# Scores of batches 2 and 3 as float32 products in row tiles, in a fused attention and feed-forward kernel

## The chip, the cores and the metric

The kernel runs on one core of one Trainium2 chip. The metric is the device time of one execution in microseconds (us). Before the change it is 682.39 us, the median of 3 runs (682.06, 682.39, 684.04). One further execution was profiled; all rows below are from it.

## The reference

Attention with 4 batches, 8 heads, 576 positions and 64 dimensions a head, and then a feed-forward layer over all 2304 tokens (512 wide, 2048 hidden):

```python
scores = np.matmul(q, k.transpose(0, 1, 3, 2)) / np.sqrt(D)
x = log1p(abs(i - j)) / log1p(max(i, 1))               # per pair of positions
scores += (np.maximum(x * w1 + b1, 0) @ w2)             # a bias per head, the same for all batches
attn = softmax(scores)                                  # over keys
x = concat_heads(attn @ v)                              # 2304 x 512
h = x @ w_in
out = (h * sigmoid(h)) @ w_out
```

All inputs but the two feed-forward weights are float32; those are float64 and are narrowed to float32 on the chip.

## The kernel before, in words

**Stages.** Work is handed out by a planner (class `Plan`, from line 202 on): every operation has a kind, an assumed duration on each engine that can do it, a due time, and the buffers it reads and writes. The due time is a time worked out from the stage's constants plus an offset from the table `SHIFT` (line 40), one for each group's loads, matmuls and other operations. The planner runs a list schedule once, in Python, and so fixes the order of the instructions on each engine. On TensorE it adds `KEEP` (1.5 us, line 214) to the due time of an operation whose kind needs the array in another mode than the last one (`MODES`, same line: the value product, the bias product, `s_row` and `s_quad` each have a mode of their own; all others share one).

Stage 1 (to about 167 us of the profiled span) builds the position bias and does attention of batches 0 and 1. Stage 2 (about 167 to 372 us) does attention of batches 2 and 3, mixed with the feed-forward steps of the first 384 tokens (`ff_block`) and the narrowing and splitting of their weights. After it come the rest of `ff_block` and three blocks of 512 tokens with a Strassen-like scheme (`ff_super`).

**Attention of one chunk** (`chunk`, line 746). For a batch, a pair of heads and 128 query positions there are two score tiles of 128 x 576, one for each head (a fifth chunk of 64 positions is done by `s_quad`, line 756, in all batches). A score tile takes two of the eight PSUM banks, and the pool for them has two slots. VectorE then adds the bias and takes the maximum (L795), ScalarE the exponential (L802), TensorE transposes (L811, 9 in a chunk, in a run of 4 and one of 5), ScalarE or VectorE copies the result out, and once in a visit of some chunks TensorE multiplies with the values (L683).

**The two ways to a score tile.** For batches in `RAW` (line 25: 0 and 1) keys are loaded once (352 KB for a pair of heads, `keys`, line 587), so that the lower 64 partitions hold the first half of the keys and the upper 64 the second half; queries stand twice. `s_row` (line 775, L779) multiplies float32 data as loaded, each half of the partitions by itself:

```python
for hf, y in enumerate(HALF):                 # partitions 0-63, 64-127
    T.matmul(out=s[:, hf, 0:288], lhsT=tl(qst)[y, ...128 columns], rhs=tl(kst)[y, ...288], ...)
```

The trace shows 4 matmul records of 64 rows for such a tile (each product is two records, and the records of the two halves start together).

For batches 2 and 3 keys are loaded as 576 KB, twice over the partitions. They are rounded to a shorter format (`k_hi`, line 599, ScalarE or VectorE, L446 or L448), and the rest is taken by a subtraction (`k_lo`, line 604, two for a pair of heads, GpSimd or VectorE, L451). Queries likewise: `q_hi` on all partitions (line 629), `q_lo` on the upper half (line 633). `s_mm` (line 783, L788) then does four products over all 128 rows:

```python
for hf in range(2):
    for j, part in enumerate((khi, klo)):
        T.matmul(out=s[:, hf, 0:288], lhsT=tl(qs)[:, ...128], rhs=tl(part)[:, ...288], start=(j == 0), stop=(j == 1))
```

Batches 2 and 3 have 64 such tiles (2 batches, 4 pairs of heads, 4 chunks, 2 heads), and so have batches 0 and 1.

**Feed-forward steps beside them.** L867 multiplies by `w_in` (128 x 384), L890 by `w_out` (128 x 512), both in the same mode as `s_mm` and the transposes. L974 and L1058 are those of `ff_super`.

Of the kernel before, what the change touches and what calls it, by code (L numbers as in the profile page):

```python
# [24 lines left out]
RAW, QUAD, WL = (0, 1), (0, 1, 2, 3), 36.0  # L25
# [10 lines left out]
def f(ap):  # L36
# [4 lines left out]
    0: -7.0, 1: 7.2, 2: -8.7, 4: -10.5, 5: -14.0, 6: -14.7, 8: -19.2, 9: -21.0, 10: -18.6, 12: -17.2,  # L41
    13: -18.5, 14: -9.8, 16: -16.4, 17: -6.4, 18: 4.7, 20: -8.1, 21: -11.7, 22: 12.8, 24: -5.2, 25: -7.1,
    26: 1.7, 28: -3.1, 29: -26.7, 30: 5.4, 32: -4.9, 33: -23.7, 34: -10.8, 36: -9.6, 37: -16.1, 38: -12.7,
    40: -6.4, 41: -8.3, 42: -11.4, 44: -24.3, 45: -29.4, 46: -28.2, 48: -5.1, 49: -9.3, 50: -0.5, 52: -23.9,
    53: -23.5, 54: -16.7, 56: -27.5, 57: -25.7, 58: -20.1, 60: 4.1, 61: -0.1, 62: 3.8, 64: 8.7, 65: 8.1,
    66: -1.9, 68: 7.8, 69: 14.7, 70: 8.1, 72: 12.6, 73: 16.4, 76: 14.4, 77: 10.2, 78: 11.6, 80: 4.6, 81: -24.7,
    82: 3.1, 84: -3.2, 85: 0.7, 86: -3.2, 88: 4.3, 89: -24.8, 90: 7.1, 92: -9.1, 93: -34.8, 94: -8.7, 96: -7.4,
    97: -22.8, 98: -22.1, 100: -13.1, 101: -10.2, 102: -9.7, 104: -0.8, 105: -0.4, 106: 2.5, 108: 1.7,
    109: 2.6, 110: 6.6, 112: 18.1, 113: 3.1, 114: 9.0, 116: 1.1, 117: -8.2, 118: -0.3, 120: -0.2, 121: -12.5,
    122: -0.4, 124: -7.9, 125: -12.6, 126: -17.3, 128: -4.0, 129: -5.3, 130: -3.7, 132: 2.8, 133: -15.5,  # L50
    134: 5.0, 136: 9.3, 137: -19.5, 138: 0.8, 140: -2.8, 141: -29.5, 142: -8.8, 144: 2.8, 145: -20.9,
    146: -22.4, 148: 8.1, 149: -12.1, 150: 14.7, 152: -14.5, 153: -7.5, 154: -4.7, 156: -0.6, 157: -2.7,
    158: 17.0, 160: -0.2, 161: -16.4, 162: 1.7, 164: -9.4, 165: -33.7, 166: 1.4, 168: -4.2, 169: -5.6,
    170: -0.1, 172: -3.4, 173: -15.3, 174: 1.8, 176: 6.5, 177: -24.9, 178: 0.9, 180: 9.8, 181: -2.1, 182: -0.4,
    184: -12.2, 185: -3.7, 186: -1.6, 188: 6.7, 189: -13.5, 190: -2.5, 192: 16.8, 193: -0.9, 194: 3.1,
    196: -0.1, 197: -9.5, 198: 5.1, 200: -5.4, 201: 0.7, 202: -0.1, 204: 4.2, 205: 5.5, 206: 12.7, 208: 8.0,
    209: 7.5, 210: 7.6, 212: 15.4, 213: 4.0, 214: 13.2, 216: 7.3, 217: 1.0, 218: 4.4, 220: -0.3, 221: -2.4,
    222: -0.8, 224: 5.9, 225: -0.1, 226: -11.2, 228: 5.7, 229: -5.8, 230: -4.1, 232: 2.7, 233: -1.6, 234: 3.1,
    236: 9.4, 237: -7.4, 238: -0.8, 240: 5.1, 241: 0.3, 242: 3.7, 244: 1.2, 245: -0.9, 246: 6.3, 248: -8.9,
    249: -8.9, 250: 7.7, 252: 3.9, 253: -8.6, 254: 5.4, 256: 7.0, 257: 0.4, 258: 12.5, 260: 2.3, 261: -1.5,  # L60
    262: -0.8, 264: 9.9, 265: -5.1, 266: 6.9, 268: 0.4, 269: -10.9, 270: -8.1, 272: 13.8, 273: -9.7, 274: 12.1,
    276: -19.9, 277: -14.6, 278: -14.1, 280: -9.1, 281: -5.9, 282: -6.8, 284: 9.7, 285: -3.1, 286: -3.8,
    288: 22.2, 289: 1.6, 290: -0.2, 292: 37.9, 293: -6.4, 294: -4.8, 296: 17.7, 297: -0.1, 298: -3.5, 300: 0.5,
    301: -11.1, 302: -6.6, 304: 13.0, 305: -18.6, 306: -2.9, 308: 9.4, 309: -2.2, 310: -3.1, 312: 13.1,
    313: -10.3, 314: -10.4, 316: 21.4, 317: 5.4, 318: -7.1, 320: -2.1, 321: -1.5, 322: -11.3, 324: 10.8,
    325: -1.6, 326: -3.4, 328: 12.6, 329: 7.1, 330: -4.9, 332: 3.7, 333: 10.8, 334: 13.6, 336: -3.8, 337: -2.4,
    338: -4.1, 340: -2.8, 341: -15.1, 342: -14.3, 344: -8.7, 345: -7.9, 346: 3.5, 348: -4.7, 349: -5.6,
    350: -0.2, 352: 8.1, 353: -3.2, 354: 10.4, 356: -3.5, 357: -5.5, 358: 1.3, 360: 4.2, 361: -2.3, 362: 4.3,
    364: -7.4, 365: -12.4, 366: -16.2, 368: -7.2, 369: -7.2, 370: -3.2, 372: 6.7, 373: 6.6, 374: 7.2,
    376: -28.6, 377: -8.5, 378: -3.2, 380: -21.8, 381: -29.9, 382: -25.2, 384: 5.4, 385: -3.5, 386: 2.6,  # L70
    388: -6.5, 389: 6.7, 390: -8.6, 392: 5.7, 393: -3.5, 394: -1.1, 396: -2.4, 397: -2.0, 398: -1.8, 400: 8.0,
    401: 13.3, 402: 8.4, 404: 16.0, 405: 1.9, 406: 5.4, 408: -11.5, 409: -5.9, 410: -11.7, 412: -7.6,
    413: -4.7, 414: -7.6, 416: -11.0, 417: -27.1, 418: -8.5, 420: -19.9, 421: -39.2, 422: -24.3, 424: 11.0,
    425: 9.8, 426: 10.4, 428: 5.5, 429: -4.9, 430: -0.8, 432: 0.4, 433: -23.5, 434: -2.0, 436: -5.2, 437: -5.4,
    438: -4.3, 440: 3.4, 441: 4.3, 442: -6.2, 444: 5.7, 445: 4.9, 446: -3.4, 448: 10.8, 449: 2.8, 450: -4.7,
    452: -10.7, 453: -13.0, 454: 8.2, 456: 16.5, 457: 2.6, 458: 10.4, 460: 1.9, 461: 3.0, 462: 1.6, 464: 13.9,
    465: 8.4, 466: 11.0, 468: 10.2, 469: 10.3, 470: 11.8, 472: 10.5, 473: 1.0, 474: 1.0, 476: 12.5, 477: 8.7,
    478: 2.3, 480: -2.4, 481: -12.5, 482: -2.7, 484: 2.0, 485: -4.3, 486: 0.2, 488: -4.9, 489: 1.5, 490: 9.4,
    492: -6.3, 493: -5.6, 494: -7.4, 496: -2.5, 497: -0.3, 498: 1.8, 500: -12.0, 501: 1.0, 502: 1.2, 505: -0.6,
    506: 1.1, 508: 7.2, 509: -4.1, 510: 0.2, 512: 1.9, 513: 1.5, 514: 6.1, 516: -15.9, 517: -15.0, 518: 4.6,  # L80
    520: -15.3, 521: -1.1, 522: 17.7, 524: -3.6, 525: -6.2, 526: 2.9, 528: 6.9, 529: -5.3, 530: 4.2,
    532: -18.5, 533: 14.7, 534: 19.5, 536: -4.2, 537: 2.7, 538: -6.9, 540: -5.7, 541: 2.2, 542: 5.2, 544: 9.5,
    545: -15.8, 546: -10.5, 548: 7.8, 549: 0.5, 550: 2.7, 552: -18.8, 553: -0.7, 554: 5.7, 556: 7.1, 557: 3.6,
    558: 7.0, 560: 23.0, 561: -1.7, 562: 1.1, 564: -6.5, 565: 3.8, 566: -6.5, 568: 1.6, 569: 0.5, 570: 20.2,
    573: -1.7, 574: -4.9, 576: 2.7, 577: -4.8, 578: -9.9, 580: 8.2, 581: 5.1, 582: -4.4, 584: 2.1, 585: -1.8,
    586: -5.8, 588: -5.7, 589: 4.1, 590: -4.6, 592: -13.8, 593: -3.1, 594: -1.9, 596: 7.8, 597: 9.7, 598: 9.0,
    600: -4.2, 601: -0.8, 602: -2.9, 604: 6.2, 605: 0.7, 606: 0.7, 608: 6.9, 609: 4.0, 610: 7.5, 612: 2.4,
    613: -0.9, 614: 6.6, 616: 11.8, 617: 3.8, 618: 0.1, 620: 15.7, 621: -5.2, 622: 16.3, 624: -2.4, 625: -3.2,
    626: 1.4, 628: 21.2, 629: 8.1, 630: 13.9, 632: 10.8, 633: 6.0, 634: 10.8, 636: 4.1, 637: 4.0, 638: -0.5,
    640: 1.9, 644: 3.4, 645: -4.7, 646: -4.0, 648: 8.4, 649: 6.6, 650: 1.6, 652: -6.4, 653: 2.1, 654: -4.1,  # L90
    656: -2.7, 657: 8.5, 658: -1.2, 660: 4.6, 661: 4.7, 662: 3.6, 664: 9.2, 665: 8.7, 666: 15.6, 668: 1.3,
    669: 3.3, 670: 4.6, 672: -1.5, 673: 2.4, 674: 9.3, 676: 4.4, 677: -2.5, 678: -0.7, 680: 0.7, 681: -1.0,
    682: -1.4, 684: 3.2, 685: -1.5, 686: -1.0, 688: -7.6, 689: 1.7, 690: -5.8, 692: 8.5, 693: 12.6, 694: 6.4,
    696: 3.9, 697: 1.3, 698: 1.6, 700: 21.6, 701: 0.7, 702: 11.1, 704: 9.4, 705: -0.6, 706: 3.6, 708: 5.9,
    709: 5.3, 710: 6.8, 712: 3.5, 713: 5.9, 714: 6.9, 716: -2.1, 717: -2.3, 718: -0.5, 720: -1.6, 721: -5.3,
    722: 0.8, 724: 0.4, 725: 0.4, 726: 4.4, 728: -4.5, 729: 6.0, 730: 6.2, 732: 14.3, 733: 18.6, 734: 20.5,
    736: 5.7, 737: 1.2, 738: -2.5, 740: 2.9, 741: 5.1, 742: 2.2, 744: -0.8, 745: 10.7, 746: 4.6, 748: -0.3,
    749: -2.7, 750: 4.0, 752: -2.8, 753: 2.1, 754: 26.5, 756: 7.7, 757: 7.6, 758: 5.6, 760: 3.6, 761: 6.3,
    762: 3.5, 764: 2.8, 765: 7.4, 766: 7.2, 768: 6.9, 769: 4.6, 770: -3.6, 772: 12.4, 773: -0.7, 774: 6.0,
    776: -12.5, 777: 0.1, 778: -3.7, 780: 9.9, 781: 6.1, 782: -2.0, 784: 15.1, 785: -1.0, 786: 7.2, 788: -0.8,  # L100
    789: -0.7, 790: -0.4, 792: 13.9, 793: 12.9, 794: 14.7, 796: 8.7, 797: 10.3, 798: -13.5, 800: -2.5,
    801: 5.6, 802: -1.3, 804: 7.8, 805: 16.3, 806: 17.2, 808: -10.1, 809: -10.5, 810: -6.5, 812: -8.0,
# [1183 lines left out]
```

## Time and profile before

| | |
|---|---|
| median of 3 runs | 682.39 us |
| the profiled execution | 683.77 us, of which the span of instructions 681.8 us |
| granted TensorE clock | 1.00 in every slice |
| busy share of the span | TensorE 98%, its weight loads 83%, VectorE 83%, ScalarE 62%, GpSimd 18% |
| moved by DMA | 186 MB, 274 GB/s |

A busy TensorE says little here: matmul records overlap, and a record lasts longer than the next one waits. What a matmul costs is read from start to start. In the rows, "L788" is line 788 of the kernel, "PEld" a weight load, and "a<-b" the tile written and those read.

### The profile page before, as it was taken

The numbers are of one execution on the slowest core, as the hardware profiler recorded it, in microseconds if no ns is written. First come the engines' busy times: TensorE is split into PE (matmuls) and PEld (weight loads), VectorE is DVE, ScalarE is ACT, GpSimd is POOL, SyncE is SP. The second block draws the span as 40 slices with busy tenths as digits, with TensorE's granted clock in tenths as the row PEclk, the third lists the DMA queues.
The fourth block names the chain that finished last, engine by engine and source line by source line (L and its number), as shares of the span: only waits on it lengthen the run. The fifth ranks groups of instructions, "written<-read, shape, count | busy, mean of one in ns | idle before, by whom it ended". The sixth has DMA issues, their size and how long they took to land.

```text
span 681.8 us, 15118 instructions
## 1 busy us (share of the span) xinstructions
PE 669.7 (98%) x5500; PEld 568.5 (83%) x5500; DVE 567.8 (83%) x1240; ACT 423.6 (62%) x901; POOL 120.6 (18%) x119
## 2 busy tenths in 40 slices
PE   9899999999999999999999999999999999999997
PEld 5356767777878788787877899999999999999997
DVE  7899696788999998898977788988899566995775
ACT  8899685678898787697755346565574423632331
POOL 1000000204241222114303223230131000300120
PEclk9999999999999999999999999999999999999999
DMA  8989846788699874889547969899899888799921
GB/s 289 313 281 317 273 136 203 242 257 259 224 332 299 314 240 161 289 257 323 158 135 258 357 253 324 303 307 309 295 361 395 289 342 283 281 372 351 402 91 62
DMA packets 84073, 186.49 MB, mean 274 GB/s; under 512 B 11552, under 2 KB 34464, under 8 KB 84000
## 3 DMA queue, kind: packets, MB, share of 16 engines
q1 hardware_dynamic: 84000, 185.54, 79.3%
q8 instruction: 43, 0.70, 0.4%
q14 instruction: 30, 0.25, 0.1%
HBM read 139.93 MB, written 45.57 MB: 272 GB/s over the span
## 4 chain that ended last, share of the span: by engine, by line
PE 56%; DVE 2%; DMA 1%; ACT 1%; issue 0%; ACTq 0%; DVEq 0%
PE psum L1058 18%; PE psum L974 17%; PE psum L867 7%; PE psum L890 6%; PE psum L683 3%; PE psum L811 2%; PE psum L788 2%; DMA G<-win_d 1%; ACT G L802 0%; PE psum L762 0%; DVE G L451 0%; ACT G L446 0%; DVE G L1037 0%; ACT w L533 0%; DVE w L546 0%
## 5 line engine op out<-in xcount | busy, mean ns | idle before, releaser
L802 ACT ACTIVATE G<-G,sm 128x576 f32<-128x576 f32 (+1 forms) x144 | 111.5, 777 | 29.5 <-DVE sm L795 28.7
L1058 PE MATMUL psum<-G 128*128 128x256 f32 x864 | 119.2, 283 | 0.3 <-DVE G L451 0.3
L795 DVE CUSTOM_DVE_ANT_0 G<-psum,G 128x576 f32<-128x576 f32 (+1 forms) x144 | 105.4, 759 | 9.5 <-PE psum L788 4.0
L1058 PEld LDWEIGHTS psum<-G 128*128 128x128 f32 x864 | 110.5, 192 | 0.7 <-DVE G L451 0.5
L811 PEld LDWEIGHTS psum<-ident,G 128*128 128x128 f32 x656 | 73.0, 141 | 25.9 <-ACT G L802 8.6
L811 PE MATMUL psum<-ident,G 128*128 128x128 f32 x656 | 91.9, 277 | 1.6 <-ACT G L802 0.8
L683 PE MATMUL psum<-pt,M 128*64 128x128 f32 (+3 forms) x1120 | 85.8, 306 | 0.2 <-ACT pt L446 0.2
L974 PE MATMUL psum<-pt,G 128*128 128x256 f32 x576 | 81.1, 284 | 0.0
L683 PEld LDWEIGHTS psum<-pt,M 128*64 128x64 f32 x1120 | 62.0, 137 | 21.9 <-issue 3.9
L867 PE MATMUL psum<-M,G 128*128 128x384 f32 x384 | 76.4, 341 | 0.0
L890 PE MATMUL psum<-G,M 128*128 128x512 f32 x288 | 75.2, 398 | 0.0
L974 PEld LDWEIGHTS psum<-pt,G 128*128 128x128 f32 x576 | 74.3, 192 | 0.6 <-ACT M L446 0.2
L451 POOL TENSOR_TENSOR G<-w,G 128x512 fp32r<-128x512 f32 x27 | 36.1, 1345 | 184.7 <-ACT G L446 158.2
L446 ACT ACTIVATE pt<-psum 128x512 f32<-128x512 f32 (+3 forms) x100 | 51.7, 535 | 26.4 <-PE psum L811 20.1
L867 PEld LDWEIGHTS psum<-M,G 128*128 128x128 f32 x384 | 65.9, 188 | 2.3 <-issue 1.0
L448 DVE COPY pt<-psum 128x640 f32<-128x640 f32 (+3 forms) x92 | 53.9, 602 | 14.2 <-PE psum L811 8.5
L890 PEld LDWEIGHTS psum<-G,M 128*128 128x128 f32 x288 | 51.6, 188 | 9.9 <-issue 1.3
L446 ACT ACTIVATE G<-G 128x512 fp32r<-128x512 f32 (+1 forms) x56 | 38.0, 694 | 23.0 <-DVE G L1037 19.5
L1010 ACT ACTIVATE M<-M 128x512 f32<-128x512 f32 x24 | 15.2, 631 | 54.4 <-DVE M L1001 54.4
L446 ACT ACTIVATE G<-w 128x512 fp32r<-128x512 f32 x64 | 39.4, 625 | 11.3 <-DVE w L551 5.4
L788 PE MATMUL psum<-G,M 128*128 128x288 f32 x256 | 45.8, 309 | 0.4 <-DVE pt L448 0.2
L788 PEld LDWEIGHTS psum<-G,M 128*128 128x128 f32 x256 | 36.6, 188 | 7.4 <-DVE sm L795 2.2
(100 smaller groups left out, 1056.7 us busy)
## 6 DMA issues: line engine op xcount, KB each, us to landing
G<-ts_d SPq DMA_DIRECT2D x48, 512.0 KB, 5.6
G<-win_d SPq DMA_DIRECT2D x40, 512.0 KB, 6.7
G<-bias_d SPq DMA_DIRECT2D x32, 576.0 KB, 5.8
G<-us_d SPq DMA_DIRECT2D x32, 512.0 KB, 6.4
bias_d<-G SPq DMA_DIRECT2D x36, 295.5 KB, 5.2
G<-in_w_out_dram SPq DMA_DIRECT2D x16, 512.0 KB, 6.0
G<-in_w_in_dram SPq DMA_DIRECT2D x16, 512.0 KB, 5.1
win_d<-G SPq DMA_DIRECT2D x16, 512.0 KB, 5.5
```

The lines of the kernel that those rows point to most:

```text
L446: A.activation(out=out, in_=in_, func=AF.Copy)
L448: ENG[e].tensor_copy(out=out, in_=in_)
L451: ENG[e].tensor_tensor(out=out, in0=in0, in1=f(in1), op=ALU.subtract)
L683: T.matmul(out=tl(o)[x, d:d + n], lhsT=tl(vs)[:, (s + 1) % 5 * 128 + 64 * a:(s + 1) % 5 * 128 + 64 * a + 64], rhs=tl(pt)[:, s + 5 * a if s ...
L788: T.matmul(out=s[:, hf, 0:288], lhsT=tl(qs)[:, x0 + 128 * a:x0 + 128 * a + 128], rhs=tl(part)[:, S * a + 288 * hf:S * a + 288 * hf + 288], ...
L795: V.tensor_tensor_reduce(out=mine(p, a).rearrange("p (a n) -> p a n", a=2), in0=tl(sps[a]).rearrange("p (a n) -> p a n", a=2)[:, :, 0:widt ...
L802: A.activation(out=mine(p, a), in_=mine(p, a), func=AF.Exp, scale=-1.0, bias=tl(sm)[:, i + a:i + a + 1], accum_out=tl(sq)[:, col + 4 * a:c ...
L811: T.transpose(out=tl(tp)[:, 128 * s:128 * s + 128], in_=tl(p)[:, 128 * (s0 + s):128 * (s0 + s) + 128], identity=ident)
L867: T.matmul(out=tl(hp)[:, 0:TB], lhsT=tl(wr)[:, x, 128 * cc:128 * cc + 128], rhs=tl(xs[cc])[:, y, :], start=(cc + m == 0), stop=(cc == NC - ...
L890: T.matmul(out=tl(acc[i]), lhsT=tl(gg)[:, x, 128 * i:128 * i + 128], rhs=tl(wo[fi])[:, y, :], start=(fi == 0 and m == 0), stop=(fi == NF - ...
L974: T.matmul(out=half(i), lhsT=tl(w)[:, x, off + 128 * cc:off + 128 * cc + 128], rhs=tl(b)[:, at, y, :], start=(fresh and cc + n == 0), stop ...
L1058: T.matmul(out=tl(c)[:, 256 * i:256 * i + 256], lhsT=tl(g)[:, a, x + 128 * i:x + 128 * i + 128], rhs=tl(w)[:, b, y:y + 256], start=(fresh ...
```

## The change

Two things are edited. `RAW` now names all four batches, so that every branch on it goes the other way for batches 2 and 3: their keys are loaded in the 352 KB layout (also at the host, which lays out `k0` for `len(RAW)` batches), `k_hi`, `k_lo`, `q_hi` and `q_lo` aren't issued, `s_row` takes the place of `s_mm`, and `s_quad` reads the keys at the offsets of the other layout. And all offsets in `SHIFT` are new; the groups keep their numbers.

```diff
-RAW, QUAD, WL = (0, 1), (0, 1, 2, 3), 36.0
+RAW, QUAD, WL = (0, 1, 2, 3), (0, 1, 2, 3), 36.0
...
 SHIFT = {
-    0: -7.0, 1: 7.2, 2: -8.7, 4: -10.5, 5: -14.0, 6: -14.7, 8: -19.2, 9: -21.0, 10: -18.6, 12: -17.2,
...
+    0: -12.3, 1: 0.7, 2: -18.9, 4: -12.3, 5: -10.8, 6: -9.9, 8: -17.3, 9: -13.7, 10: -21.1, 12: -19.4,
...
 }
```

The branches that it turns, in `keys`, `queries` and `chunk`:

```python
if b in RAW:                                   # keys: one buffer, no split
    kst = buf("G", [128, 704]); load("ld_k", ..., in_=k0[b, hp]); return kst, kst, kst
if b in RAW or not n:                          # queries: as loaded
    return qst, qst
for a in range(2) if b in RAW else (): ...     # chunk: s_row
for a in range(2) if b not in RAW else (): ... # chunk: s_mm
```

## Rows read from the trace of the kernel before

**Rows 1.** The page: engines' busy time over the span, and TensorE's granted clock in 40 slices.
```profile
PE 669.7 (98%) x5500; PEld 568.5 (83%) x5500; DVE 567.8 (83%) x1240; ACT 423.6 (62%) x901; POOL 120.6 (18%) x119
...
PEclk9999999999999999999999999999999999999999
```

**Rows 2.** Busy time by stretch, stage 2: stretch, length, then engines, clock, DMA.
```profile
167.00:207.00 40.00, 39.77 (x350) 33.32 (x351) 38.94 (x89) 35.87 (x81) 15.46 (x15) 1.00 0.82 284
...
sum 205.00, PE 204.33 PEld 166.41 DVE 184.58 ACT 157.08 POOL 52.48; mean PE 40.87 PEld 33.28 DVE 36.92 ACT 31.42 POOL 10.49
```

**Rows 3.** Timeline of TensorE, stage 1: start, length, engine, line, operands, records.
```profile
90.19 1.20 PE L811 MATMUL psum<-ident,G 128*128 128x128 f32 x9
91.33 1.24 PE L779 MATMUL psum<-G,M 64*128 64x288 f32 x8
92.50 1.20 PE L811 MATMUL psum<-ident,G 128*128 128x128 f32 x9
```

**Rows 4.** Timeline of TensorE where stage 1 passes into stage 2.
```profile
166.85 0.76 PE L779 MATMUL psum<-G,M 64*128 64x288 f32 x4
167.53 0.80 PE L788 MATMUL psum<-G,M 128*128 128x288 f32 x4
168.17 1.15 PE L811 MATMUL psum<-ident,G 128*128 128x128 f32 x9
169.07 1.31 PE L788 MATMUL psum<-G,M 128*128 128x288 f32 x8
170.24 0.77 PE L811 MATMUL psum<-ident,G 128*128 128x128 f32 x5
```

**Rows 5.** Timeline of TensorE in stage 2, score tiles between feed-forward steps.
```profile
238.11 0.69 PE L788 MATMUL psum<-G,M 128*128 128x288 f32 x4
238.64 0.70 PE L867 MATMUL psum<-M,G 128*128 128x384 f32 x3
...
240.15 1.21 PE L788 MATMUL psum<-G,M 128*128 128x288 f32 x8
241.20 0.85 PE L890 MATMUL psum<-G,M 128*128 128x512 f32 x3
```

**Rows 6.** Timeline of TensorE in stage 2, score tiles behind a value product.
```profile
257.60 1.34 PE L788 MATMUL psum<-G,M 128*128 128x288 f32 x8
258.78 0.86 PE L890 MATMUL psum<-G,M 128*128 128x512 f32 x3
```

**Rows 7.** Timeline of TensorE, the first run of row-tiled score tiles.
```profile
44.69 1.62 PE L779 MATMUL psum<-G,M 64*128 64x288 f32 x8
```

**Rows 8.** Timeline of TensorE, the last run of split score tiles.
```profile
361.67 1.22 PE L788 MATMUL psum<-G,M 128*128 128x288 f32 x8
```

**Rows 9.** Groups by line and shape, whole span: count, busy, mean ns, idle before.
```profile
L446 ACT ACTIVATE G<-G 128x1152 fp32r<-128x1152 f32 x7 | 8.1, 1153 | 0.0
L451 DVE TENSOR_TENSOR G<-G 128x576 fp32r<-128x576 f32 x11 | 8.0, 750 | 0.0
L451 POOL TENSOR_TENSOR G<-G 128x576 fp32r<-128x576 f32 x5 | 7.0, 1424 | 4.8 <-PE psum L683 3.5 <-ACT G L446 1.2
L446 ACT ACTIVATE M<-M 128x512 fp32r<-128x512 f32 x11 | 6.9, 626 | 0.4 <-DMA M<-in_q_dram 0.4
L451 DVE TENSOR_TENSOR M<-M 64x512 fp32r<-64x512 f32 x9 | 6.3, 700 | 0.5 <-ACT M L446 0.3
L451 POOL TENSOR_TENSOR M<-M 64x512 fp32r<-64x512 f32 x7 | 10.1, 1447 | 27.6 <-ACT M L446 18.5 <-DMA M<-in_q_dram 5.0 <-PE psum L762 3.7
```

**Rows 10.** Timeline of TensorE in stage 2, its largest late start inside one mode.
```profile
348.88 1.51 PE L788 MATMUL psum<-G,M 128*128 128x288 f32 x8 [0.21 <-DVE pt L448]
350.22 0.69 PE L867 MATMUL psum<-M,G 128*128 128x384 f32 x3
```

**Rows 11.** DMA issues: count, KB each, median us to landing.
```profile
G<-in_k_dram SPq DMA_DIRECT2D x8, 576.0 KB, 5.6
```

**Rows 12.** The page: the chain that ended last, share of the span by engine.
```profile
PE 56%; DVE 2%; DMA 1%; ACT 1%; issue 0%; ACTq 0%; DVEq 0%
```

298 rows, old and new, of the table SHIFT are left out of this document.

## The prediction

> **What bounds the kernel now.** I read the page first: TensorE is busy 98% of the span at the full granted clock, 2.4 GHz, the next engine (VectorE) 83% [rows 1]. Then the stretches of stage 2, where the change lies: TensorE is without a record for 0.67 of 205 us; VectorE has 184.58 us there and is nearly full only at the start, 38.94 of 40 [rows 2]. Busy records overlap, though, so third I read TensorE's timeline from start to start, to see what one tile costs and what it costs to get into and out of it. In it nearly every record of stage 2 follows the one before at the usual step of its line. I counted the starts that come over 50 ns later than that line or that pair of lines usually has: 20 in stage 2; all lateness there, the small ones too, sums to 5.0 us. One is the pair of tiles at 348.88, which takes 1.34 us to the next start [rows 10] where 1.05 is usual [rows 5]. So stage 2 is bound by the sum of TensorE's steps, and its feed-forward work fills what attention leaves: a step more on TensorE is a later end, a step less on another engine is worth only the lateness that it caused.
>
> **The change part by part.**
>
> *The products.* 64 tiles of `s_mm` go, 64 of `s_row` come. `s_mm` between feed-forward steps takes 0.53 us for one tile (238.11 to 238.64) and 1.05 for two (240.15 to 241.20) [rows 5]. `s_row` takes 0.68 us alone (166.85 to 167.53) [rows 4] and 1.17 for two (91.33 to 92.50) [rows 3], so a further tile costs 0.49, and a run has about 0.2 on top. Streaming alone gains 64 x 0.04 = 2.6 us.
>
> *The changes of mode.* Those 0.2 us, and more at the neighbours, are paid for every run of `s_row`. Beside transposes: nine of them and a pair of `s_row` take 2.31 us (90.19 to 92.50) [rows 3]; nine and a pair of `s_mm` take 2.07 (168.17 to 170.24) [rows 4]. A pair costs 0.24 more. Beside feed-forward steps no row has `s_row`, so I bound it. The pair itself is 1.17 against 1.05, +0.12. The first product behind it is slow: the tile of `s_mm` that follows `s_row` takes 0.64 (167.53 to 168.17) [rows 4] instead of 0.53, +0.11. What the step before loses by the change of mode is between nothing and the 0.24 of the transposes' both sides; with the rest of that, 0.13, the pair comes to +0.36. Ends +0.23 and +0.47. Both kinds of neighbour occur, so I take 0.28 for a pair, and 0.38 for a single tile (0.68 against 0.53, and 0.11 and 0.12 beside it). Behind a value product `s_mm` already pays: 1.18 for two (257.60 to 258.78) [rows 6], 0.13 over its usual 1.05, since the value product has a mode of its own. `s_row` there pays it in its place, so each side of a run that touches a value product or an `s_quad` saves about 0.15.
>
> The Trainium skill's page TensorEngine Tiling, section Key Properties, says that changing the tiling mode, not just the tile, drains TensorE; it gives no price. By the streaming steps alone the products would make the kernel 2.6 us faster; by the rule each run pays a drain twice, which is what the rows at the edges of L779 show.
>
> *How many runs.* With two PSUM slots a run has at most two tiles: 32 runs at least. Stage 1 has 32 runs of `s_row`, 30 of them pairs (the first at 44.69 [rows 7], the last at 166.85 [rows 4]). Stage 2 has its 64 tiles of `s_mm` in 50 runs, 36 of them single (first at 167.53 [rows 4], last at 361.67 [rows 8]): a slot comes free when VectorE has taken a maximum, and with feed-forward steps at hand a tile goes at once. The planner charges 1.5 us for a change of mode, so I go by stage 1 and take 30 pairs and 4 singles, and 12 sides at a value product or an `s_quad` (stage 2 has 16 value products and 8 `s_quad`):
>
> 30 x 0.28 + 4 x 0.38 - 12 x 0.15 = 8.4 + 1.5 - 1.8 = 8.1 us more on TensorE.
>
> Ends: 32 pairs, each with one side free, at 0.12: +3.8. Cut as now, 14 x 0.28 + 36 x 0.38: +17.6.
>
> *The splits that go.* VectorE loses 11 x 0.750 + 9 x 0.700 = 14.6 us, GpSimd 5 x 1.424 + 7 x 1.447 = 17.2, ScalarE 7 x 1.153 + 11 x 0.626 = 15.0 [rows 9] (the other 1 + 5 rounding copies ran on VectorE). None is on TensorE. They are worth the lateness of TensorE that they cause: at least nothing, at most the 5.0 us of stage 2. VectorE keeps some 170 of its 184.58 us there [rows 2], and the wait at 348.88 was for a copy that stays (L448 [rows 10]). I take half, 2.5 us. The cover of the rest is TensorE's own row of work: if TensorE were not full, up to 14.6 us would show.
>
> *The loads.* 8 loads of keys shrink from 576 KB [rows 11] to 352, 1.8 MB less; the number that SP issues stays. In the tile rows above no `s_mm` waits for keys, and none for the key buffers, of which two in three become free. Nothing, in either direction. A tile can now start when two loads have landed instead of after a copy and a subtraction; TensorE wasn't waiting for these either.
>
> *The offsets.* They change the order everywhere, and the trace doesn't show that order. Lateness counted as above is 4.2 us in 43 to 167 us, 2.4 in 372 to 520 and 4.3 before 43; new offsets can give some back or add as much. I take nothing and keep 3 us either way.
>
> **Sum.** +8.1 - 2.5 = +5.6 us. Against the profiled execution, 683.8 us with 681.8 of span, this is 689.4; that execution lies 1.4 above the median of the runs, so against the median it is **688.0 us**.
>
> **The rivals.**
>
> *The tiles stay single.* VectorE frees the score slots one at a time, and if attention is the more urgent work, TensorE takes each tile when its slot comes free, as it did in 36 of 50 runs. Price: 17.6 - 1.8 - 2.5 = +13.3, 695.7 us; half-way there 692. For it: those 36. Against: the planner's charge, and stage 1.
>
> *A draw.* The planner lays the pairs at value products and `s_quad`s (24 of them in stage 2 could cover most of 32 runs on one side): 32 x 0.12 = 3.8, and the removed splits give back 2.5 to 5: -1.2 to +1.3, so 681.2 to 683.7. Against: in stage 1, with 15 value products among 32 runs, 11 of 64 sides touched one.
>
> *Faster: the splits held TensorE up.* The place is the start of stage 2, where VectorE is at 97% [rows 2] and each score waits for a maximum in its queue, the feed-forward for weights that the same engine narrows. The chain gives VectorE 2% and ScalarE 1% of the span [rows 12], some 20 us. If the 14.6 us on VectorE were on that path, all lateness between 43 and 520 us, 4.2 + 5.0 + 2.4 = 11.6, could come back: 8.1 - 11.6 = -3.5, **678.9 us**. It decides from the point where more than 8.1 us come back. Against: stage 2 holds only 5.0 of them, and from 207 us on VectorE has room.
> The Trainium skill's page SBUF — State Buffer, section Who interferes with whom, has a VectorE instruction with two SBUF inputs and a GpSimd instruction that reads SBUF block each other; by it the 12 subtractions that leave GpSimd would also quicken what stays on VectorE. No row here separates this, and it acts through the same lateness.
>
> That the change doesn't do what it says I leave out: `s_row` runs in stage 1 with the same shapes.
>
> **How the numbers follow.** Forecast (mostly pairs, 684.5 to 692.5): 0.56. Single tiles (692.5 to 699): 0.13. Draw: 0.18. Faster: 0.13. What a measurement of this kernel can tell from no change is about 0.3%, 2 us: faster is under 680.3, slower over 684.4. Faster 0.13, within it 0.18, slower 0.69. The range leaves out most of the faster case and the worst of the single tiles: 681.0 to 694.5; the forecast's own is 684.5 to 692.5.
>
> **What would show it.** In the changed kernel, L788 is gone and L779 has 512 records. Right: L779 between 170 and 372 us in 32 to 38 runs of mostly 8 records, 1.17 us from start to next start; the feed-forward step behind such a run about 0.1 us longer than its usual step; TensorE without gaps; VectorE's busy time down by 15 to 18 us and the end later all the same; the stretch after stage 2 shifted, not shortened. Wrong in size: runs of 4 records (then later), or most runs next to L683 and L762 (then a draw). Wrong altogether: TensorE's lateness in stage 2 falls from 5.0 us to near nothing and stages 1 and 3 tighten too, so that the end comes earlier in spite of the changes of mode.

## The result, and the profile after

The changed kernel takes **691.13 us** (median of 4, 690.27 to 693.14) against 682.22 for the kernel before in the same runs (681.9 to 684.04): ratio **1.0138**, 95% interval 1.0122 to 1.0153, 8.9 us slower. The forecast was 688.0 us and slower. The profiled execution after took 691.26 us with a span of 689.5; the one before had 681.8 of span and lay 1.5 us above its median, so the spans differ by 7.7 only, and it is these 7.7 that the traces can explain.

The page after, as in [rows 1]: busy time of each engine, and TensorE's granted clock.

```profile
PE 677.0 (98%) x5500; PEld 554.2 (80%) x5500; DVE 562.5 (82%) x1222; ACT 401.0 (58%) x870; POOL 108.7 (16%) x112
...
PEclk9999999999999999999999999999999999999999
```

Same share of TensorE, same clock, as many matmul records: together they take longer. ScalarE has 22.6 us less to do and GpSimd 11.9, and the end is later all the same. Stage 2 by stretch, as in [rows 2], here up to 375 us:

```profile
167.00:207.00 40.00, 40.00 (x335) 28.14 (x333) 39.43 (x92) 34.02 (x78) 11.01 (x11) 1.00 0.86 290
...
sum 208.00, PE 206.96 PEld 148.87 DVE 179.64 ACT 137.75 POOL 47.71; mean PE 41.39 PEld 29.77 DVE 35.93 ACT 27.55 POOL 9.54
```

TensorE is as full as before, and VectorE no less so at the start (39.43 of 40, where it was 38.94). The difference is in the steps, from one start to the next. The timeline of TensorE after, row-tiled pairs between feed-forward steps (to be read against [rows 5], from start to start):

```profile
226.28 2.30 PE L890 MATMUL psum<-G,M 128*128 128x512 f32 x9
228.50 1.24 PE L779 MATMUL psum<-G,M 64*128 64x288 f32 x8
229.68 1.31 PE L867 MATMUL psum<-M,G 128*128 128x384 f32 x6
230.92 1.26 PE L779 MATMUL psum<-G,M 64*128 64x288 f32 x8
...
246.02 0.76 PE L779 MATMUL psum<-G,M 64*128 64x288 f32 x4
246.71 0.77 PE L811 MATMUL psum<-ident,G 128*128 128x128 f32 x5
```

A pair takes 1.18 us (228.50 to 229.68) where two tiles of `s_mm` took 1.05, a single 0.69 (246.02 to 246.71) where one took 0.53. Behind a value product (L683) a pair is no dearer than `s_mm` was there [rows 6], 1.17 us from 355.45 to 356.62 against 1.18:

```profile
353.14 2.38 PE L683 MATMUL psum<-pt,M 128*64 128x256 f32 x20
355.45 1.24 PE L779 MATMUL psum<-G,M 64*128 64x288 f32 x8
356.62 0.66 PE L811 MATMUL psum<-ident,G 128*128 128x128 f32 x4
```

For the whole span I split the time of TensorE, start to start, into three parts: *streaming* (the usual step of each line times its count), *changes of mode* (what the last step before a boundary between tiling modes and the first step behind it take over their usual), and *lateness* (every other start that comes later than usual). The table has all kernels of the study; "stage 2" is 167 to 375 us of each. Median and ratio are of several executions, the span and its parts of one profiled execution; the 5.4 to 5.8 us that the parts lack of the span lie before the first matmul and after the last one starts.

| kernel | median us | ratio to before, 95% | span | streaming | changes of mode (number) | lateness | of it in stage 2 |
|---|---|---|---|---|---|---|---|
| before | 682.2 | | 681.8 | 634.2 | 25.6 (162) | 16.6 | 6.5 |
| after | 691.1 | 1.0122 to 1.0153 | 689.5 | 631.1 | 38.2 (226) | 14.7 | 2.7 |
| e1 | 688.8 | 1.0088 to 1.0121 | 686.0 | 633.9 | 26.4 (165) | 20.2 | 7.6 |
| e2 | 691.4 | 1.0117 to 1.0148 | 690.3 | 630.9 | 42.1 (248) | 11.8 | 1.1 |
| e3 | 679.8 | 0.9958 to 0.9981 | 678.9 | 633.9 | 25.7 (162) | 14.0 | 4.1 |
| e4 | 704.0 | 1.0307 to 1.0340 | 703.9 | 631.6 | 41.7 (245) | 25.2 | 9.1 |
| e5 | 690.2 | 1.0095 to 1.0139 | 688.2 | 631.2 | 42.1 (248) | 9.5 | 0.9 |
| e6 | 722.8 | 1.0569 to 1.0631 | 721.7 | 631.7 | 38.4 (224) | 45.8 | 19.8 |
| e7 | 700.8 | 1.0245 to 1.0296 | 699.3 | 633.9 | 26.1 (164) | 33.5 | 10.0 |
| e8 | 704.6 | 1.0276 to 1.0352 | 704.2 | 634.5 | 26.5 (166) | 37.5 | 17.7 |
| e9 | 686.7 | 1.0054 to 1.0089 | 686.0 | 633.0 | 34.4 (207) | 13.2 | 2.8 |
| e10 | 688.1 | 1.0079 to 1.0113 | 686.9 | 634.0 | 26.1 (162) | 21.3 | 11.1 |
| e11 | 680.5 | 0.9970 to 0.9991 | 678.3 | 633.9 | 25.7 (162) | 13.3 | 4.6 |
| e12 | 687.8 | 1.0060 to 1.0113 | 686.4 | 634.2 | 25.8 (162) | 20.9 | 10.0 |

After minus before: streaming -3.1, changes of mode +12.6, lateness -1.9, together +7.6 of the 7.7 us of span. 64 changes more for 12.6 us is 0.197 us each. The sizes depend on what is taken as a usual step, by up to 1 us in a part.

### The profile page after: what moved, and what is told of

Same layout as the page of the kernel before. It is cut to its first block, busy times and chain, and to the rows that moved or that the text cites. A ratio compares the mean times of both kernels' runs of the same rounds, so it can differ in the third digit from the quotient of the medians.

```text
span 689.5 us, 15048 instructions
## 1 busy us (share of the span) xinstructions
PE 677.0 (98%) x5500; PEld 554.2 (80%) x5500; DVE 562.5 (82%) x1222; ACT 401.0 (58%) x870; POOL 108.7 (16%) x112
## 4 chain that ended last, share of the span: by engine, by line
PE 83%; DVE 6%; DMA 5%; ACT 4%; issue 1%; SPq 1%; DVEq 0%; ACTq 0%
PE psum L1058 17%; PE psum L974 17%; PE psum L811 11%; PE psum L779 10%; PE psum L683 10%; PE psum L867 9%; PE psum L890 7%; PE psum L511 2%; DMA G<-in_w_in_dram 1%; ACT G L802 1%; DMA M<-in_q_dram 1%; PE psum L762 1%; ACT G L518 1%; DVE G L505 1%; DMA G<-bias_d 1%
## 5 line engine op out<-in xcount | busy, mean ns | idle before, releaser
L802 ACT ACTIVATE G<-G,sm 128x576 f32<-128x576 f32 (+1 forms) x144 | 111.4, 777 | 38.5 <-DVE sm L795 38.2
L795 DVE CUSTOM_DVE_ANT_0 G<-psum,G 128x576 f32<-128x576 f32 (+1 forms) x144 | 104.9, 760 | 8.1 <-PE psum L779 6.2
L683 PE MATMUL psum<-pt,M 128*64 128x128 f32 (+3 forms) x1120 | 85.5, 306 | 0.0
L779 PE MATMUL psum<-G,M 64*128 64x288 f32 x512 | 82.7, 435 | 0.5 <-DVE sm L795 0.4
L448 DVE COPY pt<-psum 128x640 f32<-128x640 f32 (+3 forms) x108 | 64.9, 618 | 19.6 <-PE psum L811 12.5
L683 PEld LDWEIGHTS psum<-pt,M 128*64 128x64 f32 x1120 | 61.4, 137 | 22.9 <-issue 5.1
L867 PE MATMUL psum<-M,G 128*128 128x384 f32 x384 | 78.4, 346 | 0.0
L890 PE MATMUL psum<-G,M 128*128 128x512 f32 x288 | 73.7, 399 | 0.0
L779 PEld LDWEIGHTS psum<-G,M 64*128 64x128 f32 x512 | 42.5, 185 | 26.8 <-issue 9.9
L890 PEld LDWEIGHTS psum<-G,M 128*128 128x128 f32 x288 | 52.0, 188 | 13.7 <-issue 3.7
L446 ACT ACTIVATE pt<-psum 128x512 f32<-128x512 f32 (+3 forms) x84 | 42.4, 522 | 26.6 <-PE psum L811 19.9
L446 ACT ACTIVATE G<-G 128x512 fp32r<-128x512 f32 x51 | 31.0, 626 | 29.9 <-DVE G L1037 18.6
```

The source lines that it names most:

```text
L446: A.activation(out=out, in_=in_, func=AF.Copy)
L448: ENG[e].tensor_copy(out=out, in_=in_)
L683: T.matmul(out=tl(o)[x, d:d + n], lhsT=tl(vs)[:, (s + 1) % 5 * 128 + 64 * a:(s + 1) % 5 * 128 + 64 * a + 64], rhs=tl(pt)[:, s + 5 * a if s ...
L779: T.matmul(out=s[:, hf, 0:288], lhsT=tl(qst)[y, x0 + 128 * a:x0 + 128 * a + 128], rhs=tl(kst)[y, 416 * a:416 * a + 288], start=True, stop= ...
L795: V.tensor_tensor_reduce(out=mine(p, a).rearrange("p (a n) -> p a n", a=2), in0=tl(sps[a]).rearrange("p (a n) -> p a n", a=2)[:, :, 0:widt ...
L802: A.activation(out=mine(p, a), in_=mine(p, a), func=AF.Exp, scale=-1.0, bias=tl(sm)[:, i + a:i + a + 1], accum_out=tl(sq)[:, col + 4 * a:c ...
```

## Experiments

Ratios stand against the kernel before on the same chip, whose median beside these runs was 681.57 to 682.08 us. Where it says "old order" or "new order" every instruction stands where it stood in that kernel, and only the body of an operation differs. In e1, e3, e7 and e11 the score products of batches 2 and 3 read a constant tile, `fixed`; these four leave out the scores of the two batches, and their products wait for no load and no split. Line numbers shift with the edits: the score products are L779 or L788 in the kernels named so far, L787 in e2, L780 in e6, L792 and L797 in e9; the feed-forward step is L866 to L876, the transposes L810 to L820.

**e1: the new order, but batches 2 and 3 on the full array.** Taken from the kernel after:

```diff
-for hf, y in enumerate(HALF):
-    T.matmul(out=s[:, hf, 0:288], lhsT=tl(qst)[y, ...], rhs=tl(kst)[y, ...], start=True, stop=True)
+for hf in range(2):
+    for j in range(2):
+        T.matmul(out=s[:, hf, 0:288], lhsT=fixed[:, 0:128], rhs=fixed, start=(j == 0), stop=(j == 1))
```

> The changed kernel with its order of instructions as it is; only the products of the 64 score tiles of batches 2 and 3 are done in the full array's mode again, four of 288 columns for a tile, on a constant tile (so their scores are left out). Mode theory: the order then has 165 changes of TensorE's mode instead of 226; at 0.195 us each 11.9 us go, and streaming costs 2.9 more: 691.1 - 9.0 = 682.1 us (680 to 684). Rival, the new order and offsets are what costs: it stays at 688 to 691. Rival, the missing splits made room that the order wastes: no change either.

688.8 us, 6.7 above what was expected and inside the range of the first rival, that the order is what costs (688 to 691). Taking 61 changes of mode away saved 11.8 us of them and cost 2.8 of streaming, but 5.5 of lateness came up in their place. The timeline of e1 shows one such place, the stretch shown above of after:

```profile
226.14 1.21 PE L788 MATMUL psum<-fixed 128*128 128x288 f32 x8
227.19 1.22 PE L875 MATMUL psum<-M,G 128*128 128x384 f32 x6
228.64 1.48 PE L788 MATMUL psum<-fixed 128*128 128x288 f32 x8 [0.23 <-DVE sm L803]
229.95 1.21 PE L875 MATMUL psum<-M,G 128*128 128x384 f32 x6
```

The first pair now leaves after 1.05 us, the feed-forward step after 1.45, and the second pair waits 0.23 us for a score slot that VectorE's maximum frees. In the kernel after, the pair at the same place (230.92, above) starts without a wait. The chain that ended last shows the same at the start of stage 2. From 167 to 207 us, as shares of these 40 us by line (the view breaks the lines off), first of after, then of e1:

```profile
by line: PE psum L811 26.3%; PE psum L779 23.4%; PE psum L683 17.4%; PE psum L867 5.8%; ACT G L802 4.3%; issue 4.0%; ACT M L446 2.5%; DVE pt L448 1.8%; PE psum L762 1.7%; DVE G L451 1.7%; DVE G L795 1.7%; DVE w L551 1.5%; ACT pt L446 1.5%; 
```

```profile
by line: DVE G L803 25.7%; DVE pt L448 11.9%; issue 11.8%; ACT G L810 11.6%; DVE w L549 6.4%; DVE w L554 5.1%; ACT pt L446 4.1%; DVE w L544 3.7%; DVE w L540 3.4%; DVE G L451 3.2%; DVE M L451 2.6%; DVE sq L730 2.4%; ACT M L446 2.2%; ACT w L5
```

In after it runs mostly through TensorE, in e1 through VectorE and ScalarE. So with quick products the new order meets another bound there, and the difference between e1 and after, 2.4 us, is not the price of the products. What the new order costs by itself isn't told either: 6.7 us with full-array products (e1), about nothing with row tiles (e5 below against after).

**e2: the old order, batches 2 and 3 in row tiles, splits still made.** From the kernel before:

```diff
-for hf in range(2):
-    for j, part in enumerate((khi, klo)):
-        T.matmul(out=s[:, hf, 0:288], lhsT=tl(qs)[...], rhs=tl(part)[...], start=(j == 0), stop=(j == 1))
+for hf, y in enumerate(HALF):
+    T.matmul(out=s[:, hf, 0:288], lhsT=tl(qst)[y, ...], rhs=tl(kst)[y, S * a + 288 * hf:...], start=True, stop=True)
```

> The kernel before with its order as it is, key loads of 576 KB and all splits issued (but not read); only the 64 tiles are multiplied as float32 data in two row tiles. Mode theory: 248 changes of mode instead of 162, 86 x 0.195 = 16.8, less 2.9 of streaming: 682.2 + 13.9 = 696 us (693 to 698). Rival, offsets and order cost: 682 to 684.

691.4 us: slower by 9.3, less than expected. The timeline of e2 at the place of [rows 5]:

```profile
240.60 0.76 PE L787 MATMUL psum<-G,M 64*128 64x288 f32 x4
241.28 0.79 PE L866 MATMUL psum<-M,G 128*128 128x384 f32 x3
241.92 0.60 PE L810 MATMUL psum<-ident,G 128*128 128x128 f32 x4
242.27 0.77 PE L866 MATMUL psum<-M,G 128*128 128x384 f32 x3
242.97 1.24 PE L787 MATMUL psum<-G,M 64*128 64x288 f32 x8
244.15 0.96 PE L889 MATMUL psum<-G,M 128*128 128x512 f32 x3
```

and the two steps of before that stand between those of [rows 5]:

```profile
239.18 0.60 PE L811 MATMUL psum<-ident,G 128*128 128x128 f32 x4
239.53 0.78 PE L867 MATMUL psum<-M,G 128*128 128x384 f32 x3
```

The single takes 0.68 us for 0.53, the feed-forward step behind it 0.64 (241.28 to 241.92) for 0.54 (238.64 to 239.18), the step ahead of the pair 0.70 (242.27 to 242.97) for 0.62 (239.53 to 240.15), and the pair 1.18 for 1.05. So at this place the neighbours lose 0.10 behind a run ([rows 4] had 0.11) and 0.08 ahead of it, which no row of before showed beside a feed-forward step: 0.15 + 0.10 + 0.08 = 0.33 for a single, 0.13 + 0.18 = 0.31 for a pair, where the forecast took 0.38 and 0.28. 86 changes more cost 16.5 us, 0.192 each, and lateness fell by 4.8 us: with every split still there, that of stage 2 went from 6.5 to 1.1. The chain that ended last runs through nothing but TensorE in stage 2 of e2 (167 to 375 us):

```profile
by line: PE psum L866 21.2%; PE psum L787 19.8%; PE psum L810 19.5%; PE psum L683 19.4%; PE psum L889 17.4%; PE psum L762 2.4%; PE psum L779 0.3%; PE psum L733 0.1%
```

A stall that an engine meets anyway absorbs part of what makes the engine slower; that is why the price of the products was 9 us and not 13 (16.5 - 3.3).

**e3: the old order, the products on the full array, no splits.** The four split bodies (`k_hi`, `k_lo`, `q_hi`, `q_lo`) become `pass`, and the products read `fixed` as in e1.

> The kernel before with its order as it is, without the 8 + 16 rounding copies and the 16 + 16 subtractions; the products of the 64 tiles are as many and as long on a constant tile (their scores are left out). Mode theory with the relief as forecast: 2.5 us of TensorE's lateness come back, 679.7 us (677.2 to 682.2). Rival, the splits held TensorE up: 671 to 675. Rival, they cost nothing: 682.2.

679.8 us, as expected: all splits together, with the waits for loads that the constant tile takes away too, were worth 2.3 us. **e11** drops only the subtractions:

```diff
-sub(e, tl(klo)[...], tl(kst)[...], tl(khi)[...])
+pass
-sub(e, tl(qs)[HALF[1], :], tl(qst)[HALF[1], 0:n], tl(qs)[HALF[1], :])
+pass
```

> As the run without splits, but with the rounding copies issued: only the 32 subtractions are left out (products on a constant tile, scores of batches 2 and 3 left out). If the subtractions on VectorE and GpSimd are the 2.3 us: 680. If the copies, mostly on ScalarE, are: 682.

680.5 us, 1.3 below before: the subtractions were worth no more than that, since here too the products read `fixed` and wait for no load or copy. The two intervals overlap, so what the rounding copies were worth is not told from nothing. The engines' sums in stage 2 (167 to 375 us, columns as above), first of before, then of e3:

```profile
sum 208.00, PE 206.48 PEld 167.49 DVE 187.18 ACT 158.15 POOL 54.45; mean PE 206.48 PEld 167.49 DVE 187.18 ACT 158.15 POOL 54.45
```

```profile
sum 208.00, PE 207.57 PEld 169.07 DVE 175.27 ACT 148.91 POOL 44.62; mean PE 207.57 PEld 169.07 DVE 175.27 ACT 148.91 POOL 44.62
```

Three engines lose 31 us in this stretch, TensorE gains 1.1 of busy time: 12 us off VectorE don't become 12 us of end.

**e5: the whole change in the old order**, e2's products and e3's removed splits together.

> The change in the order of the kernel before: the 64 tiles as float32 products in two row tiles, and the 48 rounding copies and subtractions not issued; keys still come as 576 KB. Mode theory, with what the first runs measured at this order (row tiles 691.4 against 682.1, splits gone 679.8): the two add, 682.1 + 9.3 - 2.3 = 689.1 us (687.5 to 690.5), so the new offsets give the change nothing. Rival, the relief is swallowed because TensorE is behind by then: 691 to 692. Rival, the order is what makes the change slow: under 686.

690.2 us, within the range for parts that add. The two parts alone were +9.3 and -2.3, which is +7.0; together they are +8.65, with an interval of 6.5 to 9.5. So by the medians the splits are worth 0.7 to 1.2 us here and not 2.3, but the times don't tell these apart: that the slower TensorE had swallowed most of what the splits cost is likely from e2, where 1.1 us of lateness was left in stage 2, and not shown. Against the kernel after (691.1) the old order with its 248 changes is as good as the new one with 226: after saves 3.9 us of changes by this count and has 5.2 more of lateness. The new offsets bought longer runs and paid for them in waits, most of them outside stage 2 (12.0 us of lateness for 8.6). In stage 2 of e5 TensorE has a record at every moment:

```profile
sum 208.00, PE 208.00 PEld 146.82 DVE 166.50 ACT 144.33 POOL 40.17; mean PE 208.00 PEld 146.82 DVE 166.50 ACT 144.33 POOL 40.17
```

**e9: half of it.** e5's edit for batch 2 alone (`if b == 2`), batch 3 as before.

> In the order of the kernel before, batch 2 alone as float32 products in row tiles and without splits (keys still 576 KB); batch 3 as before. The whole change in this order took 690.2 us, 8.5 more than before. If the cost goes with the number of changes of mode: half of it, 686 us (685 to 687). Rival, TensorE's lateness takes up the first changes of mode for nothing: 684.5 or less, and the second half then costs 6.

686.7 us, +4.9 of the +8.65, with 45 of the 86 further changes: about in proportion. The 45 cost 8.8 us, 0.196 each. This kernel has both products in one stretch of its timeline, a single row-tiled tile and, 2 us on, a split pair:

```profile
239.24 0.76 PE L792 MATMUL psum<-G,M 64*128 64x288 f32 x4
239.92 0.80 PE L876 MATMUL psum<-M,G 128*128 128x384 f32 x3
...
241.52 1.22 PE L797 MATMUL psum<-G,M 128*128 128x288 f32 x8
242.57 0.86 PE L899 MATMUL psum<-G,M 128*128 128x512 f32 x3
```

0.68 us for one tile in row mode, 1.05 us for two on the full array.

**e4: the kernel after with the offsets of before.** Only the table `SHIFT` is put back; the planner then makes another order.

> The change without the new offsets: all four batches in row tiles, no splits, the table of offsets of before. Mode theory: 245 changes of mode instead of 162 (79 runs of row-tiled tiles instead of 32): 83 x 0.195 = 16.2, less 2.9 of streaming and about 2 of relief: 693.5 us (691 to 697), that is slower than with the new offsets. Rival, the new offsets are what costs: 682 to 685.

704.0 us. Changes of mode are nearly as many as in e2 (245 for 248), lateness is 25.2 where e2 has 11.8. The direction was right, the size was missed: the offsets of before didn't carry its order over to other operations.

**e6: fewer changes.** The two tiles of a step of batches 2 and 3 as one operation, so that no run can be single, offsets as after:

```diff
-for a in range(2) if b in RAW else ():
-    @op("s_row", ("PE", 0.484), t0 + 0.1 * a, reads=[kst, qst], writes=[sps[a]])
+for both in ((0, 1),) if b > 1 else ((0,), (1,)):
+    @op("s_row", ("PE", 0.484 * len(both)), t0 + 0.1 * both[0], reads=[kst, qst], writes=[sps[a] for a in both])
```

> The changed kernel, with both tiles of a chunk of batches 2 and 3 issued as one piece, so that no run of one tile is left in stage 2: 65 runs instead of 72 by its order, but 224 changes of mode instead of 226, since the single tiles stood next to value products or a score of the fifth chunk. Mode theory as a price per change of mode: 0.4 us less, 690.7 (689.5 to 692). Rival, a price per run as the prediction had it: 7 runs at 0.3 to 0.4, 688 to 689. Rival, waiting for two free score slots costs: over 693.

722.8 us, on the side of the last rival (over 693), but far beyond any size that was given. All runs of batches 2 and 3 are pairs now (65 runs in the kernel for 72), yet the number of changes is 224 for 226: of the 15 single runs of the kernel after from 167 us on, 9 touched a value product or an `s_quad`, which have modes of their own. A pair needs both score slots at once, and lateness tripled, 45.8 us. TensorE's largest waits in e6 (167 to 520 us; total, times, longest) are for the engines that empty PSUM:

```profile
PE psum L780 <- ACT pt L446: 4.9, 4, 1.5
PE psum L812 <- DVE sm L796: 2.0, 3, 0.9
PE psum L780 <- DVE sm L796: 1.7, 3, 1.0
```

How much of this is the wait for two slots and how much the offsets, which were not made for it, stays open.

**e7: e1's products, with the planner told of them** (an operation `s_full` of 0.585 us for batches 2 and 3, no mode of its own), offsets as after.

> As the full-array run in the new order, but the planner is told: the tiles of batches 2 and 3 are of the mode of the feed-forward and take 0.585 us, no splits, new offsets (their scores are left out). Theory that the order of the changed kernel is slow because it was planned around dear products: it comes down from 688.8 to 680 to 683. Rival, the new offsets fit only the order they were chosen for: 687 or more.

700.8 us, the rival's side: the planner, knowing the right costs, does 12 us worse than e1, whose order it had made for the wrong ones. With e4 this says that here a table of offsets fits the one set of operations that it was set for.

**e8: all subtractions planned on GpSimd.** `k_lo` and `q_lo` may go to GpSimd only, offsets as before.

> The kernel before, with the subtractions of key and query splits on GpSimd alone, so VectorE loses 20 of them (14.6 us) and GpSimd gains as many of 1.4 us. If VectorE's part of the splits was what held TensorE up, most of the 2.3 us of the run without splits comes back: 680 to 681. Rival, a GpSimd subtraction takes twice as long and the products wait for it: 683 or more. The offsets are those of before, so the order shifts a little too.

704.6 us. That is over the rival's 683, but it doesn't show the rival's cause, since the order is new as in e4. TensorE's longest wait there (167 to 520 us) is for a score slot behind VectorE, not for a subtraction:

```profile
PE psum L762 <- DVE sm L795: 3.1, 1, 3.1
```

So two runs move the subtractions and leave the order alone: **e10** sends the 20 that VectorE had to GpSimd, **e12** the 12 that GpSimd had to VectorE.

```diff
-sub(e, tl(klo)[...], tl(kst)[...], tl(khi)[...])
+sub("POOL", tl(klo)[...], tl(kst)[...], tl(khi)[...])
-sub(e, tl(qs)[HALF[1], :], tl(qst)[HALF[1], 0:n], tl(qs)[HALF[1], :])
+sub("POOL", tl(qs)[HALF[1], :], tl(qst)[HALF[1], 0:n], tl(qs)[HALF[1], :])
```

> The kernel before in its own order, all products as they are; the 20 subtractions of key and query splits that ran on VectorE run on GpSimd. Unlike the run in which the planner was told so, the order stays. If VectorE's 14.6 us are what held TensorE up, 680 to 681, faster than before. Rival, GpSimd takes 1.4 us instead of 0.75 for each and shares a port with VectorE, so tiles come late: 682.5 or more.

688.1 us, 6.3 slower though VectorE has fewer instructions, as the rival had it. (e12 has "DVE" in place of "POOL".)

> The other way round from the run with GpSimd: the kernel before in its own order, with the 12 subtractions of key and query splits that ran on GpSimd on VectorE (12 x 0.75 = 9 us more there, 17.2 less on GpSimd). If GpSimd's length and its port shared with VectorE are what makes a split late, it is a version faster than both, 680 to 681.5. If VectorE is the holder, its 9 us show: 683 to 686.

687.8 us, 5.7 slower, more than either theory gave. Both ways lateness rises, by 4.7 and 4.3 us, most or all of it in stage 2 (11.1 and 10.0 us for 6.5). Leaving out the 32 subtractions (e11) saves under 2 us, shifting a part of them costs 6: in this order the place of small work mattered more than its amount.

## Why the prediction was right, and where its sizes were off

**What bounds the kernel: right.** L788 is gone, and L779 has all the products:

```profile
L779 PE MATMUL psum<-G,M 64*128 64x288 f32 x512 | 82.7, 435 | 0.5 <-DVE sm L795 0.4
```

Stage 2 is the sum of TensorE's steps, up to its lateness. e3 takes 31 us of work from three other engines there and gets 2.3 us; e9 makes half of the tiles slower and gets 4.9 of 8.65 us of the loss; in e2 the chain of stage 2 is TensorE alone. It holds of an order that keeps the other engines ahead: in e1 the start of stage 2 hangs on VectorE.

**The changes of mode: right in mechanism and price, short in number.** The forecast charged 10.7 us gross (8.1 and the 2.6 that streaming gives) for 34 runs with 12 cheap sides, that is for 56 changes, 0.19 us each. Measured are 64 more changes at 0.197 us: +12.6. The step that was off is "how many runs": from 167 us on there are 40 (25 pairs and 15 singles; that is 65 tiles, one of them still of batch 1), with 17 cheap sides, not 30 pairs and 4 singles with 12. Nor was it the planner's charge that held the singles down, on which the forecast relied: with the same charge and the offsets of before (e4) 28 of 46 runs are single, against 36 of 50 without a charge. It is with the new offsets that they fell to 15. Between 170 and 372 us there are 38, the upper end of what was to be seen. The measured 691.1 lies nearer to the half-way value of the rival with single tiles, 692, than to 688, which lay 3.1 us low. The cheap sides were as worked out (1.17 against 1.18 at 355.45). The Trainium skill's page TensorEngine Tiling, section Key Properties, by which a change of the tiling mode drains TensorE, agrees with the traces as far as these go: they show time lost on both sides of a change, 0.10 us behind the run and 0.08 ahead of it in e2, and not what the engine does in it. The price of 0.19 to 0.20 us, the same in after, e2 and e9, is from the runs alone.

**Streaming: -3.1 us** for the -2.6 forecast (0.05 us a tile, not 0.04).

**The relief: about right in size, partly wrong in cause.** Forecast -2.5 for the splits that go. In stage 2 lateness fell by 3.8 us (6.5 to 2.7; by the tighter count of the forecast it was 5.0 before). But e2, which still makes every split, had it fall by 5.4: slower steps on TensorE give the other engines time. The splits by themselves are worth 2.3 us beside fast products (e3); beside slow ones it is 0.7 to 1.2 by the medians of e2 and e5, within their intervals. So what I called relief can for the most part be the added time itself, swallowed by waits that were there; how the 3.8 us divide in the changed kernel, whose order is another, isn't shown.

**The offsets: little, within the 3 us kept for them.** Lateness outside stage 2 rose from 10.1 to 12.0 us, +1.9, and the number of runs above hangs on them too. The sum by spans is then +12.6 - 3.1 - 3.8 + 1.9 = +7.6 for the +5.6 forecast. The medians differ by 1.2 more; the profiled execution of before lay 1.5 us above its median, that of after 0.1, which accounts for it.

**VectorE down by 15 to 18 us: wrong.** It fell by 5.3 only. The new plan moved copies of transposed tiles to it from ScalarE. The groups of after, then the same two of before (count, busy, mean ns, idle before):

```profile
L448 DVE COPY pt<-psum 128x640 f32<-128x640 f32 x43 | 35.3, 820 | 6.7 <-PE psum L811 5.5 <-ACT pt L446 1.0
L446 ACT ACTIVATE pt<-psum 128x640 f32<-128x640 f32 x21 | 14.7, 702 | 6.4 <-PE psum L811 4.6 <-issue 1.1 <-PE psum L683 0.5
```

```profile
L448 DVE COPY pt<-psum 128x640 f32<-128x640 f32 x31 | 25.4, 820 | 3.5 <-PE psum L811 3.0 <-ACT pt L446 0.2
L446 ACT ACTIVATE pt<-psum 128x640 f32<-128x640 f32 x33 | 23.2, 702 | 8.1 <-PE psum L811 7.7 <-PE psum L683 0.5
```

12 copies more at 820 ns are 9.9 us. Room on VectorE alone doesn't do it: in e4, without splits but with the offsets of before, these copies stay where they were:

```profile
L448 DVE COPY pt<-psum 128x640 f32<-128x640 f32 x30 | 24.6, 819 | 6.2 <-PE psum L811 3.6 <-PE psum L683 2.4 <-ACT pt L446 0.2
L446 ACT ACTIVATE pt<-psum 128x640 f32<-128x640 f32 x34 | 24.0, 705 | 10.6 <-PE psum L811 7.5 <-PE psum L683 2.8
```

What the move cost, no run shows by itself.

**The stretch after stage 2: shifted, and a little longer.** The last `s_quad` comes 5.4 us later (375.9 for 370.5), the end 7.7. The chain that ended last has these shares of the span:

```profile
PE 83%; DVE 6%; DMA 5%; ACT 4%; issue 1%; SPq 1%; DVEq 0%; ACTq 0%
```

They are not to be set against [rows 12], whose shares sum to 60%: the chain of before can be followed back only to its first piece at 268 us, and the shares are still of the whole span:

```profile
268.17 0.04 issue
```

In the part that it covers, TensorE has 56 of the 60.

**The rivals.** *Faster* needed over 8.1 us from the splits; e3 gives all that they hold, 2.3, and e11 says that the subtractions hold under 2 of it. The forecast read the place of this rival, the start of stage 2, from [rows 12], whose chain doesn't reach it; in e1, where the rival's bound does show up there, it was the new order with fast products that brought it. *A draw* needed the runs laid at value products and `s_quad`s: 17 of 80 sides were, and 64 changes remain. *The tiles stay single* came true by half, as said above. *The loads* are as said, 352 KB for the 576 of [rows 11], and no wait of TensorE hangs on them:

```profile
G<-in_k_dram SPq DMA_DIRECT2D x16, 352.0 KB, 6.1
```

No version here that computes the whole result beats the kernel before.

## What to carry to other kernels

Where TensorE is the bound, count how often a new product changes its tiling mode before counting what it streams: here 64 tiles gained 3 us of streaming and paid 0.2 us at each of 64 more changes. Work on engines beside the bound is worth only the stalls that it causes (2.3 us here for some 47 us of splits [rows 9]), and a slower bound swallows stalls by itself (e2: 13.2 us of longer steps became 8.5 us of span), so a gain measured beside the fast bound need not come back beside the slow one. And test a part of a change in the old order of instructions: replanning with offsets made for other operations cost 12 to 17 us here (e4, e7, e8, each against the kernel with the same work in an order that was kept), which hides every effect of this size.

## What the runs showed that I had not expected

VectorE's instructions with two SBUF inputs became slower when GpSimd subtracted more. In e10, stage 2 (167 to 375 us; count, busy, mean ns, idle before):

```profile
L795 DVE CUSTOM_DVE_ANT_0 G<-psum,G 128x576 f32<-128x576 f32 x65 | 47.6, 751 | 3.3 <-PE psum L788 3.0 <-ACT pt L446 0.2
...
L546 DVE SCALAR_TENSOR_TENSOR w<-G,w 128x512 uint32<-128x512 uint32 x28 | 22.8, 820 | 0.3
L551 DVE SCALAR_TENSOR_TENSOR w<-G,w 128x512 uint32<-128x512 uint32 x28 | 22.4, 805 | 0.2
```

and the same lines of the kernel before in the same stretch:

```profile
L795 DVE CUSTOM_DVE_ANT_0 G<-psum,G 128x576 f32<-128x576 f32 x66 | 48.5, 751 | 4.6 <-PE psum L788 4.0 <-ACT pt L446 0.2 <-PE psum L779 0.2
...
L546 DVE SCALAR_TENSOR_TENSOR w<-G,w 128x512 uint32<-128x512 uint32 x28 | 19.5, 704 | 0.2
L551 DVE SCALAR_TENSOR_TENSOR w<-G,w 128x512 uint32<-128x512 uint32 x28 | 19.1, 687 | 0.2
```

L546 goes from 704 to 820 ns and L551 from 687 to 805, while the maximum L795, one of whose inputs is in PSUM, stays at 751. So with 20 subtractions taken from VectorE, 56 other instructions there take 6.6 us longer in all. This agrees with the Trainium skill's page SBUF — State Buffer, section Who interferes with whom, by which a VectorE instruction with two SBUF inputs and a GpSimd instruction that reads SBUF block each other. The other way, with no subtraction of scores on GpSimd (e12), L546 takes 686 ns: the 12 that were there had cost little. And the changed kernel, which has none of them either, gained nothing by this path; the same two lines of after in stage 2 are longer than before, not shorter:

```profile
L546 DVE SCALAR_TENSOR_TENSOR w<-G,w 128x512 uint32<-128x512 uint32 x28 | 20.3, 725 | 0.4
L551 DVE SCALAR_TENSOR_TENSOR w<-G,w 128x512 uint32<-128x512 uint32 x28 | 19.5, 700 | 0.3
```
